# One transformer block on one core: w1 and the last V are summed in 64-row tiles, in two passes with the row halves swapped

## The chip, the cores and the metric

The kernel runs on one core of one Trainium2 chip. The metric is device time in microseconds (us), smaller is better. Before the change three runs took 169.43, 171.04 and 171.4 us; the median is 171.04 us.

The engines of the core are TensorE (PE for its matmuls, PEld for the loads of their stationary operand), VectorE (DVE), ScalarE (ACT), GpSimd (POOL) and SyncE (SP, which here issues the DMAs). Each engine works through its own list of instructions in order, and they wait for each other through semaphores.

## The reference

S is 2048, D is 448, there are 16 heads of 28, and F is 1792. `c` is turned into six modulation vectors of 448.

```python
h = _layernorm(x) * (1 + ca) + sa
x = x + ga * attention(h, wqkv, wo)       # each position sees 8 keys at distances 0, 2, .., 14
h = _layernorm(x) * (1 + cb) + sb
y = _layernorm(h)
x = x + gb * (gelu(y @ w1 + b1) @ w2 + b2)
```

Every product of a 448-wide row with a matrix (q, k, v, w1) sums over 448 = 3 * 128 + 64 rows of the stationary operand. The product with w2 sums over 1792 = 14 * 128.

## The kernel before

The even and the odd positions are two streams (`n` or `s`, 0 and 1), each 1024 long, so a dilated window is an ordinary window inside one stream. A `p` (0 to 7) is 128 positions of both streams, a `t` (0 to 3) is two of these.

The work has three stretches that repeat. **The front** (to about 63 us) loads x and the weights, normalises, forms hT (the transposed rows), q, k and v, and runs attention for the first five of nine batches. **Attention** of a batch `i` is `pv` (v), two `lt` (logits), an exp on ACT, a mask on DVE, `pd` (denominators), `po` (values) and a multiplication on DVE. `out_proj` of a `p` (tile `pw`) adds to x and normalises again into `yT`. **The MLP** of a `t` has fourteen `p1` sums (w1: seven pairs g, of which each has two outputs a in the two banks of one PSUM tile), one GELU on ACT for each output, which writes a slice of `hm`, and then `p2` (w2). Four MLPs follow each other, with the attention batches left over between the first three.

How 448 rows are summed: a matmul over 128 rows uses the whole array. For the last 64 rows the two halves of the array work at the same time: one matmul takes rows 0 to 63 for one output and another takes rows 64 to 127 for the other output. That is the tile shape 64x128 instead of 128x128. `summed()` does this: `full()` (line 548) issues three 128-row matmuls for each output, `rest()` (line 554) one 64-row matmul for each output, side by side in pairs. The operands' 64 last rows lie in both halves for this (`w1_r`, and the last part of `yT` and `hT`).

What sets the order: every piece of work is a task of a `Plan` with its engine, inputs and buffers. The order in which tasks are written out is the list `ORDER`, and the buffer of each tile is in the list `SLOTS`; both are fixed numbers in the file. The PSUM has four tiles of two banks (room "P"), shared by all of pq, pv, lt, pd, po, pw, p1 and p2. A task `12:A` of ORDER runs on ACT instead of its usual engine.

Lines of the profile that the text below names: 548 (128-row matmuls of q, k, v, w1), 554 (their 64-row matmuls), 706 (`pv` of the first five batches), 738 (`lt`), 760 (`pd`), 771 (`po`), 803 (`pw`), 883 (`p2`), 864 (GELU), 609 (q and k out of PSUM), 504 (hT), 661 (w2 scaled by gb on DVE), 456 and 458 (statistics), 469 (a power on POOL), 478 (normalisation), 819 (modulation), 889 (last sum). A program has shortened tile names in the profile: `p` is p1 at lines 548 and 554 and p2 at line 883, `w_s` is w1_s or w2_s, `w_r` is w1_r, `h` is h2.

Of the kernel before, what the change touches and what calls it, by code (L numbers as in the profile page):

```python
# [57 lines left out]
192 273:A 162 157 189 171 308:D 194 172 283 193 244 218 173 195 163 219 158 275 284 196 216 285 167 217 286 447:P 246
197 164 168 165 228 174 169:D 274 309 312 276:D 277 220 313 310 314 166 221 229 225 230 311 224 222:D 247 170 315 245
176 317 316 175 226 248 233 232 318 227 290 249 289:A 319 43 287:A 223 288 320 234 250 558:P 46 45 559 321 47 231 253  # L60
345 342 346 251 560 303 482:P 44 252 324 343 322 291 561 254 323 325 347 326 344 292 304 255 293 327 348 328 373:R 256
305 294 329 257 350 258 375 52 378 376 330 340:R 53 333 379 235 377 374 296 334 331 300 41 295 351 332 259 49 335 380
299 341 336 337 297 260 382 262 301 381 349 263 261 264 338:A 383 483 352 339 384 265 484 266 449 353 267 485 385 268
# [3 lines left out]
402 452 404 443 487 453 370 490 454 444 436 455 371:D 372 456 434 491 405 488 457 493 445 459 458 492 460 435 494 461  # L67
# [3 lines left out]
513 547 515:D 599 516 564 602 568 481 569 570 604 603 571 546 605 572 548 606 573 628 607 608 574 549 635 575 550 609  # L71
612 636 577 630 637 578 610 629 640 576 579 638 581 639 611 613 580 582 641 631 583 633 586 651 614 632 587 584 585
616 588 642 615 648 617 654 646 647 618 634 652 645 656 621 649 619 644 622 620 623 643 658 650 625 624 589 626 664
590 655 627 591:A 653 657 439 592 659 556 665 662 663 674 666 660 661 669 667 675 668 678 676 679 677 686 672 673 671
687 681 670 680 690 691 694 697 693 682 688 692 685 695 683 689 701 684 698 696 709 699 710 702 711 712 705 700 703
706 704 707 708
# [77 lines left out]
def kernel(  # L154
# [14 lines left out]
    nc = tc.nc  # L169
# [3 lines left out]
    P = Plan()  # L173
# [368 lines left out]

    def summed(items, slot, reads, bufs, fills, name, after=(), split=None):
# [70 lines left out]
    def natural_qk(p):  # L614
        c0 = LEAD + 128 * p
        for half in (1, 0):
            pq = psum("pq")

            def item(s, half=half, pq=pq):
                return (lambda: pq.t[:, s, 0:D], lambda kt, rows: hT[rows, NS * kt + s, c0:c0 + 128],  # L620
                        lambda kt, rows: (wqk_st.t[:, kt] if kt < KT - 1 else wqr_st.t[rows])[:, half * D:half * D + D])

            summed([item(s) for s in range(NS)], 0.1895, [f"wqk{k}" for k in range(KT - 1)] + ["wr0", "wr1"] + [f"h{kt}_{p}" for kt in range(KT)],
                   [pq, wqk_st, wqr_st], [pq], f"qk{p}_{half}n")
# [53 lines left out]
    def attention(i, tbl, prev_w1):  # L678
# [5 lines left out]
        if i not in DIRECT:  # L684
# [10 lines left out]
            summed([(lambda s=s: pv.t[:, s, 0:D], lambda kt, rows, s=s: hw.t[rows, kt, s].rearrange("p j c -> p (j c)"),  # L695
# [101 lines left out]
    def out_proj(p):  # L797
        pw = psum("pw")

        def mm():  # L800
            for s in range(NS):
                for ft in range(4):
                    nc.tensor.matmul(pw.t[:, s, 0:D], lhsT=qT[:, KT * s + ft, LEAD + 128 * p:LEAD + 128 * p + 128], rhs=wo_s[:, ft, :],  # L803
                                     start=(ft == 0), stop=(ft == 3))

        batches = [i for i in range(NB) if i * SBQ < 128 * (p + 1) and (i + 1) * SBQ > 128 * p]
        add("PE", 8 * 0.1895, mm, reads=["wos0", "wos1"] + [f"o{i}" for i in batches], bufs=[pw], fills=[pw],
            instr=16, name=f"wo{p}")
# [36 lines left out]
    def mlp(t, tbl, lts):  # L845
        yT = yT_of[t]
        hm = sb("hm", [128, FT, NS, 256], BF16, "hm")
        for gs in ((0, 1), (2, 3), (4, 5), (6,)):
            p1s = {g: psum("p1") for g in gs}

            def item(g, a, p1s=p1s):
                def lhs(kt, rows):
                    c0 = (g + FH * a) * 128
                    return w1_s[rows, kt, c0:c0 + 128] if kt < KT - 1 else w1_r[rows, g * 128:g * 128 + 128]

                return lambda: p1s[g].t[:, a, :], lhs, lambda kt, rows: yT.t[rows, kt:kt + KT + 1:KT, :]

            w1_mms.extend(summed([item(g, a) for g in gs for a in range(2)], 0.2160,
                                 [f"w1{k}" for k in (0, 1, 2, "r0", "r1")] + [(yT, 0), (yT, 1)],
                                 [yT] + list(p1s.values()), list(p1s.values()), f"w1_{t}_{gs[0]}", after=lts))  # L860
# [10 lines left out]
        for q in range(2):  # L871
# [5 lines left out]
            for ns, c0, c1 in (([0], 0, D), ([1], 0, D // 2), ([1], D // 2, D)) if last else (([0, 1], 0, D),):  # L877
                p2, n0, n1 = psum("p2"), ns[0], ns[-1] + 1
                for n in ns:
                    for k, fs in enumerate(parts):  # L880
                        def mm(n=n, fs=fs, q=q, p2=p2, c0=c0, c1=c1):
                            for f in fs:
                                nc.tensor.matmul(p2.t[:, n, 0:c1 - c0], lhsT=hm.t[:, f, n, q * 128:(q + 1) * 128], rhs=w2_s[:, f, c0:c1],  # L883
                                                 start=(f == parts[0][0]), stop=(f == parts[-1][-1]))

                        add("PE", len(fs) * ((c1 - c0) / 2400 + 0.0025), mm, reads=[(hm, f) for f in fs] + [f"w2_{i}" for i in sorted({f // 2 for f in fs})],
                            bufs=[hm, p2], writes=[(p2, n)], instr=2 * len(fs), name=f"w2_{p}_{n}_{k}" + ("b" if c0 else ""))
# [3 lines left out]
                    bufs=[p2, x1p], reads=[(p2, n) for n in ns] + [(x1p, n) for n in ns], writes=[f"out{p}{n0}{c0}"] + ([] if last else [f"x{p}"]), name="fin")  # L891
# [71 lines left out]
```

## Time and profile before

| | |
|---|---|
| time, three runs | 169.43, 171.04, 171.4 us (median 171.04) |
| span of the profiled execution, first to last instruction | 166.6 us |
| PE busy | 160.9 us (97%) in 2126 matmuls |
| DVE busy | 116.1 us (70%) |
| ACT busy | 102.4 us (61%) |
| POOL busy | 46.7 us (28%) |
| TensorE clock granted, mean | 0.998 |

The profile covers one execution. Its span is its own time, as far as the profile gives one; what the timed runs have beyond it (171.04 - 166.6 = 4.4 us at the median) lies around the span. Busy time is the union of an engine's instructions. Matmuls overlap: each is shown from its start to the end of its results, some 0.38 us for 512 columns, while the next one starts 0.216 us after it. So the distance between two starts is what a matmul costs, not its shown duration.

### The profile page before, as it was taken

How to read it: one execution, taken by the hardware profiler on the slowest of the kernel's cores; microseconds unless marked ns; L12 is line 12 of the kernel's file. 1: busy time of each engine (PE TensorE's matmuls, PEld its weight loads, DVE VectorE, ACT ScalarE, POOL GpSimd, SP SyncE). 2: the span in 40 equal slices, each digit the busy share in tenths (PEclk: the TensorE clock that was granted, in tenths of full speed). 3: DMA queues.
4: the chain of work that ended last, by engine and by line, in shares of the span. 5: the costliest groups of instructions: out<-in, count | busy, mean ns of one | idle time of the engine just before them, and what ended most of it. 6: DMA issues, size and time to landing. Idle time of an engine off the chain costs nothing.

```text
span 166.6 us, 4971 instructions
## 1 busy us (share of the span) xinstructions
PE 160.9 (97%) x2126; PEld 83.7 (50%) x2126; DVE 116.1 (70%) x271; ACT 102.4 (61%) x142; POOL 46.7 (28%) x73
## 2 busy tenths in 40 slices
PE   6999899999999999999999999999999999999992
PEld 4678544444545543445555344556434455344572
DVE  6889899958899989996938886574788930500032
ACT  3378898798489953859674468947536820097300
POOL 3136332300261201289100114700002870007200
PEclk9999999999999999999999999999999999999999
DMA  5999989799999999900091000009010026110003
GB/s 152 323 335 311 182 269 172 147 160 190 222 185 306 147 161 245 151 0 6 2 139 46 4 0 0 4 0 126 8 55 0 0 55 185 64 46 0 0 1 110
DMA packets 35573, 18.78 MB, mean 113 GB/s; under 512 B 28507, under 2 KB 34592, under 8 KB 35552
## 3 DMA queue, kind: packets, MB, share of 16 engines
q1 hardware_dynamic: 35548, 18.47, 51.0%
q8 instruction: 16, 0.26, 0.7%
q14 instruction: 5, 0.04, 0.1%
q10 hardware_dynamic: 4, 0.00, 0.0%
HBM read 9.81 MB, written 1.84 MB: 70 GB/s over the span
## 4 chain that ended last, share of the span: by engine, by line
PE 88%; DMA 4%; ACT 2%; SPq 2%; POOL 1%; DVE 1%; issue 1%
PE p L883 26%; PE p L548 22%; PE pq L548 8%; PE pw L803 8%; PE pv L706 5%; PE p L554 4%; PE lt L738 4%; PE po L771 3%; PE pv L548 3%; DMA wqk_st<-in_A_wqkv_dram 3%; PE pq L554 2%; DMA kT<-zy 2%; PE pd L760 1%; SPq L349 1%; PE pb L641 1%
## 5 line engine op out<-in xcount | busy, mean ns | idle before, releaser
L864 ACT ACTIVATE hm<-p,b_col 128x512 bf16<-128x512 f32 x56 | 33.9, 692 | 29.9 <-PE p L554 27.3
L883 PE MATMUL p<-w_s,hm 128*128 128x448 bf16 (+1 forms) x238 | 44.1, 342 | 0.0
L548 PE MATMUL p<-yT,w_s 128*128 128x512 bf16 x168 | 38.1, 380 | 0.0
L469 POOL TENSOR_TENSOR rs_all<-mvs,neg_half 128x2 f32<-128x2 f32 x22 | 16.7, 764 | 58.0 <-DVE mvs L458 57.9
L883 PEld LDWEIGHTS <-hm 128*128 128x128 bf16 x238 | 22.6, 98 | 19.3 <-issue 0.8
L889 DVE TENSOR_TENSOR x_all<-p,x1p 128x896 bf16<-128x896 f32 (+2 forms) x10 | 8.9, 902 | 25.9 <-PE p L883 25.9
L548 PEld LDWEIGHTS <-w_s 128*128 128x128 bf16 x168 | 15.8, 98 | 20.9 <-issue 2.9
L456 DVE BATCH_NORM_STATS2 stt<-x_all 128x6 f32<-128x448 bf16 x32 | 18.6, 608 | 0.8 <-DMA x_all<-in_A_x_dram 0.6
L745 ACT ACTIVATE et<-lt 128x928 bf16<-128x928 f32 x18 | 16.0, 947 | 4.2 <-PE lt L738 3.9
L841 POOL TENSOR_TENSOR x1p<-x_all,gbb_bc 128x448 f32<-128x448 bf16 x16 | 17.8, 1137 | 0.0
L548 PE MATMUL pq<-wqk_st,hT 128*128 128x448 bf16 x72 | 15.0, 354 | 0.0
L788 DVE TENSOR_TENSOR qT<-po,den 128x912 bf16<-128x912 f32 x9 | 10.0, 1106 | 6.6 <-ACT den L782 6.4
L751 DVE TENSOR_TENSOR et<-et,mask 128x928 bf16<-128x928 bf16 x18 | 11.8, 683 | 3.1 <-ACT et L745 3.0
L803 PE MATMUL pw<-wo_s,qT 128*128 128x448 bf16 x64 | 13.3, 353 | 0.0
L780 ACT ACTIVATE den<-pd 128x928 f32<-128x928 f32 x9 | 8.5, 943 | 5.9 <-PE pd L760 5.7
L819 DVE TENSOR_TENSOR h<-h,mod_bc 128x896 bf16<-128x896 bf16 x16 | 11.1, 710 | 0.3
L628 ACT CAST zy<-pq 128x896 bf16<-128x896 f32 x10 | 8.9, 912 | 1.7 <-PE pq L554 0.9
L548 PEld LDWEIGHTS <-hT 128*128 128x128 bf16 x72 | 6.4, 98 | 6.9 <-issue 1.6
L782 ACT ACTIVATE den<-den,den_bias 128x928 f32<-128x928 f32 x9 | 9.6, 1072 | 0.2
L478 DVE TENSOR_SCALAR zy<-h,mvs,rs_all 128x448 bf16<-128x448 bf16 x16 | 6.6, 457 | 4.4 <-POOL rs_all L469 4.4
L810 DVE TENSOR_TENSOR x_all<-pw,x_all 128x896 bf16<-128x896 f32 x8 | 8.7, 1086 | 1.3 <-PE pw L803 1.3
L456 DVE BATCH_NORM_STATS2 stt<-h 128x6 f32<-128x448 bf16 x16 | 9.4, 612 | 0.2
(115 smaller groups left out, 182.0 us busy)
## 6 DMA issues: line engine op xcount, KB each, us to landing
w_s<-in_B_w_dram SPq DMA_DIRECT2D x7, 224.0 KB, 3.8
out_dram<-x_all SPq DMA_DIRECT2D x7, 224.0 KB, 2.1
x_all<-in_A_x_dram SPq DMA_DIRECT2D x3, 448.0 KB, 5.3
wmod<-in_w_mod_dram SPq DMA_DIRECT2D x3, 448.0 KB, 7.2
w_s<-in_B_w_dram SPq DMA_DIRECT2D x3, 448.0 KB
wqk_st<-in_A_wqkv_dram SPq DMA_DIRECT2D x3, 225.0 KB, 3.9
wm_st<-in_w_mod_dram SPq DMA_DIRECT2D x1, 672.0 KB, 4.6
x_all<-in_A_x_dram SPq DMA_DIRECT2D x2, 224.0 KB, 2.6
```

The costliest lines, as they stand in the source:

```text
L456: add("DVE", 0.53, lambda: nc.vector.bn_stats(out=stt[:, w, b, 0:6], in_=src()), reads=reads, bufs=bufs, after=early if w == b == 0 else ( ...
L469: ways = {"POOL": (0.55 + 0.17 * n, lambda: nc.gpsimd.tensor_tensor(out=r, in0=v, in1=neg_half[:, 0:n], op=ALU.pow))}
L548: nc.tensor.matmul(out(), lhsT=lhs(kt, slice(0, 128)), rhs=rhs(kt, slice(0, 128)), start=first and kt == 0, stop=not first and kt == KT - 2)
L554: nc.tensor.matmul(out(), lhsT=lhs(KT - 1, rows), rhs=rhs(KT - 1, rows), start=first, stop=not first, tile_position=(rows.start, 0))
L745: exps.append(add("ACT", 0.83, lambda half=half, lt=lt: nc.scalar.activation(out=et.t[:, 2 * half:2 * half + 2].rearrange("p r m c -> p r ...
L751: nc.vector.tensor_tensor(out=ev, in0=ev, in1=mask[:], op=ALU.mult)
L788: nc.vector.tensor_tensor(out=qT[:, :, LEAD + q00:LEAD + q00 + 2 * WQ], in0=po.t[:, :, 0:NS * 4 * WQ].rearrange("p j (m c) -> p m j c", c=WQ),
L803: nc.tensor.matmul(pw.t[:, s, 0:D], lhsT=qT[:, KT * s + ft, LEAD + 128 * p:LEAD + 128 * p + 128], rhs=wo_s[:, ft, :], start=(ft == 0), sto ...
L819: add("DVE", 0.55, lambda vec=vec, op=op: nc.vector.tensor_tensor(out=h2.t[:], in0=h2.t[:], in1=vec.unsqueeze(1).to_broadcast([128, NS, D] ...
L841: add("POOL", 1.0, lambda n=n: nc.gpsimd.tensor_tensor(out=x1p.t[:, n, :], in0=xn(p, n), in1=gbb2_bc[:], op=ALU.add), reads=[f"x{p}", "gbb ...
L864: gelus.append(add("ACT", 0.585, lambda f=f, a=a, p1=p1s[g]: nc.scalar.activation(out=hm.t[:, f].rearrange("p n c -> p (n c)"), in_=p1.t[: ...
L883: nc.tensor.matmul(p2.t[:, n, 0:c1 - c0], lhsT=hm.t[:, f, n, q * 128:(q + 1) * 128], rhs=w2_s[:, f, c0:c1], start=(f == parts[0][0]), stop ...
```

## The change

`paired()` takes the place of `summed()` for all w1 sums (two outputs each) and for the v of the last batch (`PAIRED_V = range(8, 9)`). All of its matmuls have the tile shape 64x128, two side by side. In the first pass, rows 0 to 63 work for output 0 and rows 64 to 127 for output 1, over all four parts of the 448 rows (the last part lies in both halves): 8 matmuls. In the second pass the halves change places, over the first three parts: 6 matmuls. Each output has then seen each of its rows once.

[...] For this there is a "hop": an instruction without work on SP, POOL, ACT or DVE that waits for the last matmul of the first pass and then signals; the first weight load of the second pass waits for that signal. ORDER says on which engine each hop runs. There are 29: 8 on DVE, 8 on POOL, 8 on SP, 5 on ACT. Between the two passes of one sum stands work of other sums.

```diff
+PAIRED_QK, PAIRED_V, PAIRED_WO, PAIRED_W2 = range(0), range(8, 9), range(0), range(0)
...
+    def swapped(first, bufs, second):
+        ends = []
+        def hop(e):
+            nop = e.nop()
+            for mm in ends:
+                link(mm, nop)
+            ends.append(nop)
+        a = first(ends)
+        b = add("SP", 0.05, lambda: hop(nc.sync), needs=a, name="hop", alt={"POOL": (0.05, lambda: hop(nc.gpsimd)), "ACT": (0.05, lambda: hop(nc.scalar)),
+                                                                           "DVE": (0.05, lambda: hop(nc.vector))})
+        return a + second(ends, [b])
...
+    def paired(items, slot, reads, bufs, fills, name, after=(), rest=True):
+        n = KT - 1 if rest else KT
+        seen = []
+        def half(first, ends):
+            start, mm = not seen, None
+            seen.append(1)
+            for kt in range(KT if first else n):
+                for a in range(2):
+                    out, lhs, rhs = items[a if first else 1 - a]
+                    rows = slice(KS * a, KS * a + KS)
+                    mm = nc.tensor.matmul(out(), lhsT=lhs(kt, rows), rhs=rhs(kt, rows), start=start and kt == 0,
+                                          stop=not start and kt == n - 1, tile_position=(rows.start, 0))
+                    if not first and kt == a == 0:
+                        link(ends[-1], mm)
+            if first:
+                ends.append(mm)
...
-            summed([(lambda s=s: pv.t[:, s, 0:D], lambda kt, rows, s=s: hw.t[rows, kt, s].rearrange("p j c -> p (j c)"),
+            (paired if i in PAIRED_V else summed)([(lambda s=s: pv.t[:, s, 0:D], lambda kt, rows, s=s: hw.t[rows, kt, s].rearrange("p j c -> p (j c)"),
...
-            w1_mms.extend(summed([item(g, a) for g in gs for a in range(2)], 0.2160,
+            for g in gs:
+                w1_mms.extend(paired([item(g, a) for a in range(2)], 0.2160, [f"w1{k}" for k in (0, 1, 2, "r0", "r1")] + [(yT, 0), (yT, 1)],
+                                     [yT, p1s[g]], [p1s[g]], f"w1_{t}_{g}", after=lts))
```

The same function could be used for q and k, for `pw` and for `p2`; those switches are empty ranges, so there the program is built as before. ORDER and SLOTS are new numbers throughout, and the order has moved on every engine. In the line numbers of the changed kernel, 548 is 592, 554 is 598, the matmuls of `paired()` are 576, the hop is 551, 609 is 653, 661 is 705, 706 is 750, 738 is 782, 864 is 915, 883 is 957 and 889 is 963.

**PE at the first MLP.** Before, around the first w1 sums (`p1_1587`, `p1_1594`, `p1_1613`; 1534 is the number of this yT):

```order
L548 LDWEIGHTS w1_s_76 [waits DMAHW5_49,DMAHW4_49,DMAHW7_49]
L548 MATMUL p1_1587<-yT_1534,w1_s_76 128x512 [waits Activation_49]
...
L548 MATMUL p1_1594<-yT_1534,w1_s_76 128x512 [waits DVE_49]
...
L554 LDWEIGHTS w1_r_77 [waits DMAHW1_49]
L554 MATMUL p1_1613<-yT_1534,w1_r_77 128x512 [waits DVE_49]
...
L548 MATMUL p1_1613<-yT_1534,w1_s_76 128x512
```

Now, at the same place (`p1_1580`, `p1_1593`, `p1_1608`; all tile shape 64x128):

```order
L576 MATMUL p1_1608<-yT_1524,w1_s_76 128x512
L576 LDWEIGHTS w1_r_77
L576 MATMUL p1_1608<-yT_1524,w1_r_77 128x512
L576 LDWEIGHTS w1_s_76 [waits Pool_sequencer_49]
L576 MATMUL p1_1580<-yT_1524,w1_s_76 128x512
...
L576 LDWEIGHTS w1_s_76 [waits DVE_sequencer_49]
L576 MATMUL p1_1593<-yT_1524,w1_s_76 128x512
```

Before, twelve 128-row matmuls, then eight 64-row ones, then 128-row ones again: two changes of shape. Now the first passes of 1580, 1593 and 1608 stand behind each other, then the second pass of 1580, whose first weight load waits for the hop on POOL, then that of 1593, which waits for the hop on DVE; the shape does not change.

**DVE during the first MLP.** Before, from the sum behind the last `pw` on (L810; `w2_s` rows scale two of the fourteen slices of w2 each):

```order
L810 TENSOR_TENSOR x_all_68<-pw_1570,x_all_68 128x896 [waits PE_49]
...
L661 TENSOR_TENSOR w2_s_78<-w2_s_78,mod_bc_82 128x896 [waits DMAHW7_49]
...
L456 BN_STATS stt_105<-h2_1607 128x6 [waits DVE_49]
L478 TENSOR_SCALAR h2_1665<-x_all_68,mvs_106,rs_all_107 128x448 [waits Pool_49]
...
L661 TENSOR_TENSOR w2_s_78<-w2_s_78,mod_bc_82 128x896 [waits DMAHW2_49]
```

Now, around its second hop (the hop itself is not a row; its wait for PE is listed with the row behind it):

```order
L733 COPY hw_1629<-hT_69 128x1024 [waits PE_49]
...
L481 TENSOR_SCALAR h2_1656<-x_all_68,mvs_106,rs_all_107 128x448 [waits Pool_49]
L705 TENSOR_TENSOR w2_s_78<-w2_s_78,mod_bc_82 128x896 [waits PE_49,DMAHW4_49]
L481 TENSOR_SCALAR h2_1643<-x_all_68,mvs_106,rs_all_107 128x448
L870 TENSOR_TENSOR h2_1643<-h2_1643,mod_bc_82 128x896 [waits DVE_49]
L705 TENSOR_TENSOR w2_s_78<-w2_s_78,mod_bc_82 128x896 [waits DMAHW7_49]
...
L705 TENSOR_TENSOR w2_s_78<-w2_s_78,mod_bc_82 128x896 [waits DMAHW1_49]
```

In both the scaling of w2 is mixed with the normalisation for the next MLP. Now DVE has two hops in it: one ahead of the copy into `hw_1629` (after the first pass of `p1_1593`) and one ahead of the scaling that waits for DMAHW4 (after the first pass of `p1_1667`). Seven scalings there are in both; three come ahead of the second hop and four behind it.

**PE in the front.** Before, at the q and k of the second `p` (`pq_353`, `pq_362`) and the start of attention (`lt_391`, `pv_447`):

```order
L548 MATMUL pq_362<-hT_69,Wqk_72 128x256
...
L554 MATMUL pq_362<-hT_69,Wqr_73 128x256
L554 MATMUL pq_353<-hT_69,Wqr_73 128x256
...
L738 MATMUL lt_391<-qT_70,kT_71 64x58 [waits PE_49]
...
L548 MATMUL pq_353<-hT_69,Wqk_72 128x256
...
L706 MATMUL pv_447<-Wv_74,hT_69 64x448 [waits Activation_49]
```

Now, at the same place (`pq_350`, `pq_365`, `lt_376`, `lt_410`, `pv_482`):

```order
L598 MATMUL pq_350<-hT_69,Wqr_73 128x256
...
L598 MATMUL pq_365<-hT_69,Wqr_73 128x256
...
L782 MATMUL lt_376<-qT_70,kT_71 64x58 [waits Activation_49]
...
L782 MATMUL lt_410<-qT_70,kT_71 64x58
...
L592 MATMUL pq_365<-hT_69,Wqk_72 128x256
...
L750 MATMUL pv_482<-Wv_74,hT_69 64x448 [waits Activation_49]
```

The two `lt` of the first batch now stand together, and ahead of them there are six 128-row matmuls and two pairs fewer; those come behind them. On ACT, `kT` is now copied out ahead of `qT`, and two parts of hT for the third `p` are formed there instead of one.

More of the change, by code (lines that the diff above doesn't have):

```diff
@@ L58 @@
[L58 to L62, printed above, removed]
@@ L77 @@
+732:P 725 738 714 728 743 739:A 715 744 740 729:D 745 733 730 746 736 748 737 747 734 742 762 735 750 741 749 763 751
+754 752 764 753 755 765 758 756 759 757 760 761
 """
@@ L620, in item @@
                 return (lambda: pq.t[:, s, 0:D], lambda kt, rows: hT[rows, NS * kt + s, c0:c0 + 128],
-                        lambda kt, rows: (wqk_st.t[:, kt] if kt < KT - 1 else wqr_st.t[rows])[:, half * D:half * D + D])
-            summed([item(s) for s in range(NS)], 0.1895, [f"wqk{k}" for k in range(KT - 1)] + ["wr0", "wr1"] + [f"h{kt}_{p}" for kt in range(KT)],
+                        lambda kt, rows: (wqk_st.t[rows, kt] if kt < KT - 1 else wqr_st.t[rows])[:, half * D:half * D + D])
+            (paired if p in PAIRED_QK else summed)([item(s) for s in range(NS)], 0.1895, [f"wqk{k}" for k in range(KT - 1)] + ["wr0", "wr1"] + [f"h{kt}_{p}" for kt in range(KT)],
                    [pq, wqk_st, wqr_st], [pq], f"qk{p}_{half}n")
@@ L798, in out_proj, with item @@
         pw = psum("pw")
+        def item(s):
+            return (lambda: pw.t[:, s, 0:D], lambda ft, rows: qT[rows, KT * s + ft, LEAD + 128 * p:LEAD + 128 * p + 128],
+                    lambda ft, rows: wo_s[rows, ft, :])
         def mm():
             for s in range(NS):
+                out, lhs, rhs = item(s)
                 for ft in range(4):
-                    nc.tensor.matmul(pw.t[:, s, 0:D], lhsT=qT[:, KT * s + ft, LEAD + 128 * p:LEAD + 128 * p + 128], rhs=wo_s[:, ft, :],
-                                     start=(ft == 0), stop=(ft == 3))
+                    nc.tensor.matmul(out(), lhsT=lhs(ft, slice(0, 128)), rhs=rhs(ft, slice(0, 128)), start=(ft == 0), stop=(ft == 3))
         batches = [i for i in range(NB) if i * SBQ < 128 * (p + 1) and (i + 1) * SBQ > 128 * p]
-        add("PE", 8 * 0.1895, mm, reads=["wos0", "wos1"] + [f"o{i}" for i in batches], bufs=[pw], fills=[pw],
-            instr=16, name=f"wo{p}")
+        reads = ["wos0", "wos1"] + [f"o{i}" for i in batches]
+        if p in PAIRED_WO:
+            paired([item(s) for s in range(NS)], 0.1895, reads, [pw], [pw], f"wo{p}", rest=False)
+        else:
+            add("PE", 8 * 0.1895, mm, reads=reads, bufs=[pw], fills=[pw], instr=16, name=f"wo{p}")
         xp = x_all[:, p, :].rearrange("p (s d) -> p s d", s=NS)
@@ L878, in mlp, with sums, half, mm @@
                 p2, n0, n1 = psum("p2"), ns[0], ns[-1] + 1
[L879 to L887, printed above, removed]
+                if p in PAIRED_W2:
+                    count = []
+                    def sums(k, up, ends, q=q, p2=p2, count=count):
+                        mm, fs, done = None, parts[k], len(count)
+                        count.append(k)
+                        for f in fs:
+                            for a in range(2):
+                                n, rows = (1 - a if up else a), slice(KS * a, KS * a + KS)
+                                mm = nc.tensor.matmul(p2.t[:, n, 0:D], lhsT=hm.t[rows, f, n, q * 128:(q + 1) * 128], rhs=w2_s[rows, f, :],
+                                                      start=done == 0 and f == fs[0], stop=done == 3 and f == fs[-1], tile_position=(rows.start, 0))
+                                if done == 2 and f == fs[0] and a == 0:
+                                    link(ends[-1], mm)
+                        if done == 1:
+                            ends.append(mm)
+                    def half(up, ends, needs=(), p=p, p2=p2, sums=sums):
+                        return [add("PE", len(parts[k]) * 0.1895, lambda k=k, sums=sums: sums(k, up, ends), instr=4 * len(parts[k]), mode="64x128", needs=needs,
+                                    reads=[(hm, f) for f in parts[k]] + [f"w2_{i}" for i in sorted({f // 2 for f in parts[k]})],
+                                    bufs=[hm, p2], joins=[p2], name=f"w2_{p}_{'lh'[up]}{k}") for k in range(2)]
+                    swapped(lambda ends: half(False, ends), [p2], lambda ends, b: half(True, ends, b))
+                else:
+                    for n in ns:
+                        for k, fs in enumerate(parts):
+                            def mm(n=n, fs=fs, q=q, p2=p2, c0=c0, c1=c1):
+                                for f in fs:
+                                    nc.tensor.matmul(p2.t[:, n, 0:c1 - c0], lhsT=hm.t[:, f, n, q * 128:(q + 1) * 128], rhs=w2_s[:, f, c0:c1],
+                                                     start=(f == parts[0][0]), stop=(f == parts[-1][-1]))
+                            add("PE", len(fs) * ((c1 - c0) / 2400 + 0.0025), mm, reads=[(hm, f) for f in fs] + [f"w2_{i}" for i in sorted({f // 2 for f in fs})],
+                                bufs=[hm, p2], writes=[(p2, n)], instr=2 * len(fs), name=f"w2_{p}_{n}_{k}" + ("b" if c0 else ""))
@@ L890, in mlp @@
                     out=xo(xi), in0=p2.t[:, n0:n1, 0:w], in1=xo(x1p.t), op=ALU.add),
-                    bufs=[p2, x1p], reads=[(p2, n) for n in ns] + [(x1p, n) for n in ns], writes=[f"out{p}{n0}{c0}"] + ([] if last else [f"x{p}"]), name="fin")
+                    bufs=[p2, x1p], reads=[(p2, n) for n in ns if p not in PAIRED_W2] + [(x1p, n) for n in ns], writes=[f"out{p}{n0}{c0}"] + ([] if last else [f"x{p}"]), name="fin")
                 lo, hi = n0 * D + c0, (n1 - 1) * D + c1
```

42 lines of the change are left out of this document (28 added, 14 removed), and 18 rows, old and new, of tables (ORDER, SLOTS).

## The prediction

> **What bounds the kernel now.** I read the head of the page first, then the busy times by stretch, then the waits, and only then single stretches of the timeline.
>
> ```profile
> span 166.6 us, 4971 instructions
> PE 160.9 (97%) x2126; PEld 83.7 (50%) x2126; DVE 116.1 (70%) x271; ACT 102.4 (61%) x142; POOL 46.7 (28%) x73
> ```
>
> PE is busy for all but 5.7 us of the span. The stretches (start:end, length, then PE, PEld, DVE, ACT and POOL busy, clock granted, DMA share, GB/s) say where these 5.7 us are:
>
> ```profile
> 0.00:12.40 12.40, 10.61 (x108) 7.66 (x108) 9.81 (x52) 5.57 (x13) 3.54 (x15) 1.00 0.87 269
> 12.40:29.00 16.60, 16.05 (x336) 9.72 (x335) 15.55 (x44) 14.07 (x20) 6.26 (x13) 1.00 1.00 236
> 29.00:45.00 16.00, 15.60 (x331) 7.75 (x332) 12.98 (x21) 11.94 (x14) 2.43 (x3) 1.00 0.91 174
> 45.00:62.90 17.90, 17.89 (x334) 9.11 (x321) 16.92 (x40) 15.52 (x19) 4.75 (x6) 1.00 1.04 202
> 62.90:73.90 11.00, 11.00 (x58) 4.46 (x56) 10.85 (x25) 5.85 (x10) 4.20 (x6) 1.00 0.81 144
> ...
> 153.00:166.60 13.60, 10.65 (x71) 6.59 (x68) 2.50 (x4) 2.44 (x5) 2.03 (x3) 0.98 0.10 34
> ```
>
> 1.79 us lie in the first 12.4 us, where weights arrive and which the change does not touch; 0.55 + 0.40 + 0.01 = 0.96 us in the rest of the front; none from 62.9 to 153; 2.95 us behind the last matmul. So nothing but the length of PE's own stream, and those 0.96 us, can be shortened. The longest wait of the front is the only one over 0.4 us:
>
> ```profile
> PE pv L706 <- ACT qT L609: 0.5, 1, 0.5
> ```
>
> **The stream of w1.** Twelve 128-row matmuls in a row, and a place where the shape changes:
>
> ```profile
> 94.76 2.75 PE L548 MATMUL p<-yT,w_s 128*128 128x512 bf16 x12
> ...
> 64.74 0.81 PE L548 MATMUL p<-yT,w_s 128*128 128x512 bf16 x3
> 65.49 1.04 PE L554 MATMUL p<-yT,w_r 64*128 64x512 bf16 x8
> 66.45 0.39 PE L548 MATMUL p<-yT,w_s 128*128 128x512 bf16 x1
> ```
>
> The last of the twelve takes 0.38 us to the end of its results (a group's mean of 380 ns stands in a row below), so the other eleven lie (2.75 - 0.38) / 11 = 0.2155 us apart. I call this a slot. Three matmuls should take 0.647 us, but the next group starts 0.75 us after them; four pairs should take 0.862 us, but take 0.96. So a pair of 64-row matmuls costs one slot, and **each change of shape about 0.10 us** more (0.095 when it is averaged over more of them).
>
> Before, two outputs cost 2 x 3 full slots and one pair: 7 slots. Now they cost (8 + 6) / 2 = 7 pair slots. For 28 pairs of outputs that is 28 x 7 x 0.2155 = 42.2 us both times: the new shape saves nothing by itself, and the 174 further matmuls (w1 392 for 224, the last V 14 for 8) lie in the other half of the same slots. What it does save is changes of shape. Counted in the order of PE's two programs there are 79 before and 73 now: seven fewer in the MLPs, one more in the front. **Term 1: -6 x 0.095 = -0.57 us.** It is small because the 64-row blocks of w1 were already collected to three or four pairs. Bounds: -0.6 to 0; zero if the pairs lose as much in another way.
>
> That pairs keep the pace over more than four of them is not shown for 64-row tiles, but for another half tile, 128x64, whose sixteen matmuls start at 20.01 and whose successor starts at 21.58 (rows further down): 1.57 us for eight pairs of 448 columns, against 8 x 0.2155 x 448/512 = 1.51 and one change of shape. The same row of instructions can be taken quickly enough:
>
> ```profile
> 84.09 1.21 PE po L771 x128
> ```
>
> That is 9.4 ns for each matmul with its weight load. [...]
>
> **The hops.** A second pass starts when the first has ended, another engine has noticed, and PE has noticed that. Each step from its row:
>
> ```profile
> L548 PE MATMUL p<-yT,w_s 128*128 128x512 bf16 x168 | 38.1, 380 | 0.0
> ...
> 163.68 0.39 DVE L889 TENSOR_TENSOR x_all<-p,x1p 128x224 bf16<-128x224 f32 x1 [0.72 <-PE p L883]
> ...
> 153.02 10.64 PE p L883 x70
> ```
>
> 0.38 us to the results; 153.02 + 10.64 = 163.66 to 163.68, 0.02 us from PE's end to another engine's start; and (rows below) ACT's cast from 17.01 to 18.02, PE's `pv` at 18.07: 0.05 us back. The hop itself does no work; I put its own time at 0.02 to 0.06 us by the shortest DVE rows, an estimate. So some **0.49 us** from the start of the last matmul of a first pass to the first weight load of the second. By the new order, seven of the 29 hops have three slots of other w1 work between the passes (0.65 us), seven have four (0.86 us), fifteen have six or more. A load may come up to one slot ahead of its matmul, so an undisturbed hop has at least 0.16 us to spare and costs nothing: the cover is the other sums' slots. If this cover were gone, a hop would cost 0.49 - 0.2155 = 0.27 us, 29 of them 8 us.
>
> But a hop stands in its engine's queue, and ahead of it may be an instruction of 0.7 to 1.1 us. Of the fourteen short ones five are on SP, four on DVE, three on POOL, two on ACT. Between 62.9 and 73.9 us ACT is busy 5.85 and POOL 4.20 of 11 us, DVE 10.85. So I charge DVE's four: half of a 0.73 us instruction (0.36) less the spare 0.16 to 0.37 gives about 0.1 each, and SP's five, which may stand behind a DMA's issue, little less. **Term 2: +0.25 us** for all, which is near the lower end; bounds 0 and +4 (all fourteen 0.3 us late).
>
> **DVE in the first MLP.** Here it was full, and w2 has to be scaled in time:
>
> ```profile
> 72.60 1.15 DVE L661 TENSOR_TENSOR w_s<-w_s,mod_bc 128x896 bf16<-128x896 bf16 x2
> 73.80 0.73 PE L883 MATMUL p<-w_s,hm 128*128 128x448 bf16 x3
> ```
>
> The last scalings ended at 73.75 and the first w2 matmul began at 73.80, without delay. Now DVE stands still at its second hop until the first pass of `p1_1667` is done. What follows it, up to the sixth scaling, is three scalings, two normalisations and two modulations:
>
> ```profile
> L661 DVE TENSOR_TENSOR w_s<-w_s,mod_bc 128x896 bf16<-128x896 bf16 x7 | 4.9, 726 | 0.0
> L478 DVE TENSOR_SCALAR h<-x_all,mvs,rs_all 128x448 bf16<-128x448 bf16 x16 | 5.8, 384 | 1.8 <-POOL rs_all L469 1.6
> L819 DVE TENSOR_TENSOR h<-h,mod_bc 128x896 bf16<-128x896 bf16 x16 | 11.1, 710 | 0.3
> ```
>
> 3 x 0.726 + 2 x 0.384 + 2 x 0.710 = 4.37 us, begun 0.42 us after the last matmul's start, so ready for PE at 4.84. PE has twenty pair slots (4.31 us), 32 small `lt` matmuls (0.37) and two changes of shape (0.19) behind that slot before the first w2: 0.22 + 4.87 = 5.09. **Term 3: 0**, with 0.25 us to spare. Bounds 0 and +1.4.
>
> **The front.** PE and ACT around the first attention, before:
>
> ```profile
> 14.70 0.49 PE L548 MATMUL pq<-hT,Wqk 128*128 128x256 bf16 x3
> 15.12 0.61 PE L554 MATMUL pq<-hT,Wqr 64*128 64x256 bf16 x8
> 15.66 0.44 PE L738 MATMUL lt<-qT,kT 28*64 28x58 bf16 x32
> 16.04 1.48 PE L548 MATMUL pq<-hT,Wqk 128*128 128x256 bf16 x12
> 18.07 1.64 PE L706 MATMUL pv<-Wv,hT 128*64 128x448 bf16 x16 [0.55 <-ACT qT L609]
> 19.64 0.44 PE L738 MATMUL lt<-qT,kT 28*64 28x58 bf16 x32
> 20.01 1.64 PE L706 MATMUL pv<-Wv,hT 128*64 128x448 bf16 x16
> 21.58 0.70 PE L738 MATMUL lt<-qT,kT 28*64 28x58 bf16 x64
> ...
> 13.55 1.02 ACT L609 CAST qT<-pq 128x1024 bf16<-128x1024 f32 x1
> 14.44 1.04 ACT L609 CAST kT<-pq 128x1024 bf16<-128x1024 f32 x1
> 17.01 1.01 ACT L609 CAST qT<-pq 128x1024 bf16<-128x1024 f32 x1
> 21.40 0.81 ACT L504 ACTIVATE hT<-zT,mod_col 128x512 bf16<-128x512 bf16 x1
> ```
>
> The first `lt` needs both casts, which end at 15.48; it started at 15.66, so it hardly waited. Now six 128-row matmuls and two pairs of 256 columns fewer stand ahead of it, 8 x 0.108 = 0.87 us (0.108 is half a slot). It is up at 14.79 and must wait to 15.53: 0.74 us new. The 0.87 us of work come behind it and use up what was the 0.55 us wait at 18.07; what is left at that `pv` is 0.74 - 0.55, some +0.15. Then the second part of hT that ACT now forms (0.81 us, in a stretch where ACT is busy 14.07 of 16.60) makes the next q and k late by what I put at 0.3. **Term 4: +0.4 us.** Bounds: -0.55, if the `pv` wait goes and nothing takes its place, and 0.74 + 0.3 = +1.0. The last V's two passes have four slots between them and cost nothing by the same cover as w1.
>
> **The sum:** -0.57 + 0.25 + 0 + 0.4 = +0.1 us. The profiled span becomes 166.7; with the 4.4 us by which the median stands above the span, 171.1 us. The tail (w2, last sum, store) is as it was.
>
> **The rivals.**
>
> - *Hops come late (slower).* An engine passes a hop only when what stands ahead of it has finished, so that PE, which never waited between 62.9 and 153 us, now does. For it: DVE's 10.85 of 11.00. Against it: ACT and POOL are half idle, and 15 hops have 1.3 us or more. Price 14 x 0.3 = +4.2 in place of 0.25: 175 us. It decides from a mean lateness of 0.24 us at these fourteen on. Chance 0.10.
> - *DVE's hop holds back w2.* The 1.4 us in which DVE stands still are not made up, and the first w2 matmul waits for a scaling: +1.3, 172.4 us. For it: no slack before; against it: the 0.25 us above. Chance 0.09.
> - *The front's waits go.* All of the 0.96 us vanish and hops are free: -0.57 - 0.96 = -1.5, 169.5 us. Chance 0.10.
> - [...] Chance 0.01.
> - *Faster by more than 2%.* 3.4 us, which is about what a measurement of this kernel can tell from no change, would need more than all waits and all the changes of shape that go (1.5 us): something I do not see. Chance 0.04.
>
> The forecast has the remaining 0.66. The range: from 169.5 with 0.8 us for the spread of the runs (169.43 to 171.4) down to 168.7, and from 172.4 with the front at its upper bound (+0.6) and a few late hops up to 173.5. Slower by over 2% takes the late hops and the slow pace, 0.11; within 2% the forecast, w2 and the front, 0.85.
>
> **What would show it.** Changes of shape: in the MLPs PE's stretches of w1 come out some 0.14 us shorter each. Hops: PE waits on SP, DVE, POOL or ACT at the `paired` line, in sum about 0.25 us; over 3 us of them is the first rival. w2: a wait of the first `p2` for DVE. Front: a wait of 0.7 us at the first `lt` instead of that at `pv`. I am wrong if a long run of 64-row pairs does not keep 0.2155 us for a slot, or if engines pass hops much later than they pass waits now.

## The result: 3% slower, and the profile after

Four runs of the changed kernel took 175.01 to 176.63 us, median 175.24, beside 170.71 for the kernel before: a ratio of **1.031 (95% interval 1.025 to 1.037)**. The forecast was 171.1, its range 168.7 to 173.5. The time lies where the first rival put it (175), but not for that rival's reason, so that this is luck.

The head of the page of the changed kernel, and its busy times by stretch (the columns are as in the prediction):

```profile
span 173.0 us, 5358 instructions
...
PE 160.9 (93%) x2300; PEld 84.3 (49%) x2300; DVE 119.3 (69%) x271; ACT 103.2 (60%) x144; POOL 46.3 (27%) x71
```

```profile
12.40:29.00 16.60, 14.59 (x250) 8.45 (x252) 13.86 (x43) 12.98 (x19) 5.97 (x11) 1.00 0.93 209
29.00:45.00 16.00, 14.69 (x355) 7.88 (x354) 12.19 (x20) 13.13 (x16) 0.64 (x2) 1.00 0.97 164
45.00:66.87 21.87, 20.73 (x384) 10.04 (x384) 20.94 (x42) 15.35 (x18) 5.74 (x7) 1.00 0.87 169
...
76.90:98.90 22.00, 20.11 (x374) 10.54 (x372) 17.08 (x28) 12.59 (x15) 8.33 (x8) 1.00 0.31 47
...
108.50:126.40 17.90, 17.47 (x350) 9.31 (x348) 12.56 (x22) 12.45 (x14) 7.20 (x9) 1.00 0.27 32
...
137.20:148.50 11.30, 10.62 (x56) 5.29 (x55) 5.84 (x11) 3.74 (x7) 3.02 (x4) 1.00 0.53 88
148.50:159.20 10.70, 10.70 (x99) 4.71 (x100) 1.51 (x2) 5.51 (x9) 2.75 (x4) 1.00 0.17 64
```

PE's busy time is the same 160.9 us. The whole loss of 6.4 us of span is time in which PE stands still: 2.0 + 1.3 + 1.1 us in the front, where it was 0.96, and 1.9 + 0.4 + 0.7 us behind it, where it was nothing. The fourth w1 (the last row) has no idle time and is shorter, 10.70 us for 11.00. Before:

```profile
142.00:153.00 11.00, 11.00 (x58) 4.54 (x56) 2.09 (x2) 6.08 (x10) 2.14 (x4) 1.00 0.11 42
```

What PE waited for, by line (us in total, times, longest):

```profile
PE pd L804 <- DVE et L795: 1.6, 2, 1.1
PE pq L592 <- ACT hT L507: 1.3, 1, 1.3
...
PE pw L852 <- DVE qT L832: 0.8, 1, 0.8
PE p L957 <- issue: 0.7, 1, 0.7
PE p L576 <- DMA yT<-zy: 0.7, 1, 0.7
PE lt L782 <- ACT qT L653: 0.7, 1, 0.7
PE pq L598 <- DVE vb L768: 0.7, 1, 0.7
PE lt L782 <- DMA qT<-zy: 0.6, 1, 0.6
```

No wait for a hop is among them: the only wait of the paired line 576 is for `yT`, at the start of the fourth MLP. Instead the engines that carry hops waited for PE:

```profile
POOL rs_all L472 <- PE p L576: 2.0, 1, 2.0
DVE w_s L705 <- PE p L576: 1.8, 1, 1.8
DVE mvs L461 <- PE p L576: 1.5, 1, 1.5
```

From the starts of matmuls in the traces:

| us | before | after | difference |
|---|---|---|---|
| first w1 matmul (end of the front) | 62.80 | 66.71 | +3.9 |
| from there to the first w1 matmul of the fourth MLP | 79.06 | 81.80 | +2.7 |
| from there to the end of the last matmul | 21.79 | 21.49 | -0.3 |

These differences compare two single executions. The text ahead of the prediction puts all of the 4.4 us by which the median time of before exceeds its profiled span outside the span. The later runs list time and span of every execution, and there only 1.7 us lie outside it (2.0 for the changed kernel). The executions of before have spans from 166.4 us up, with a median of 168.2 to 168.6 us in each set of runs: the profiled one is among the shortest. The four of the changed kernel have a median of 173.25 us. So between medians the loss is some 4.9 us instead of 6.4: the trace of before lies 1.6 to 2.0 us below its median, that of the changed kernel 0.25.

In the front there is no hop at all; it was only reordered. So three questions follow: what the front lost, what the middle lost, and what the pairs cost by themselves.

### The profile page after: what moved, and what is told of

It is laid out like the page before. It is cut to its first block, busy times and chain, and to the rows that moved or that the text cites. A ratio compares the mean times of both kernels' runs of the same rounds, so it can differ in the third digit from the quotient of the medians.

```text
span 173.0 us, 5358 instructions
## 1 busy us (share of the span) xinstructions
PE 160.9 (93%) x2300; PEld 84.3 (49%) x2300; DVE 119.3 (69%) x271; ACT 103.2 (60%) x144; POOL 46.3 (27%) x71
## 4 chain that ended last, share of the span: by engine, by line
PE 44%; DVE 23%; DMA 10%; ACT 7%; issue 6%; POOL 6%; SPq 2%; POOLq 0%; DVEq 0%; ACTq 0%
PE p L576 20%; PE p L957 11%; DVE stt L459 5%; PE pw L852 3%; DVE et L795 3%; DVE h L870 3%; POOL rs_all L472 3%; DVE zy L481 3%; DMA yT<-zy 3%; DMA wqk_st<-in_A_wqkv_dram 2%; DMA mod_bc<-mod_hbm 2%; DMA zT<-zy 2%; PE pq L592 2%; ACT hT L507 2%; PE po L815 2%
## 5 line engine op out<-in xcount | busy, mean ns | idle before, releaser
L576 PE MATMUL p<-yT,w_s 64*128 64x512 bf16 x336 | 41.5, 376 | 0.7 <-DMA yT<-zy 0.7
L576 PEld LDWEIGHTS <-w_s 64*128 64x128 bf16 x336 | 16.2, 94 | 20.6 <-DMA yT<-zy 1.1
L892 POOL TENSOR_TENSOR x1p<-x_all,gbb_bc 128x448 f32<-128x448 bf16 x16 | 18.4, 1171 | 0.1
L795 DVE TENSOR_TENSOR et<-et,mask 128x928 bf16<-128x928 bf16 x18 | 12.6, 723 | 4.2 <-ACT et L789 4.2
L870 DVE TENSOR_TENSOR h<-h,mod_bc 128x896 bf16<-128x896 bf16 x16 | 12.5, 780 | 0.4
L765 ACT CAST vb<-pv 128x896 bf16<-128x896 f32 x7 | 6.2, 901 | 7.8 <-PE pv L576 5.1
L576 PE MATMUL p<-yT,w_r 64*128 64x512 bf16 x56 | 10.6, 376 | 0.0
L852 PEld LDWEIGHTS <-qT 128*128 128x128 bf16 x64 | 6.1, 98 | 7.3 <-DVE qT L832 1.9
```

The source lines that it names most:

```text
L576: mm = nc.tensor.matmul(out(), lhsT=lhs(kt, rows), rhs=rhs(kt, rows), start=start and kt == 0, stop=not start and kt == n - 1, tile_positi ...
L795: nc.vector.tensor_tensor(out=ev, in0=ev, in1=mask[:], op=ALU.mult)
L852: nc.tensor.matmul(out(), lhsT=lhs(ft, slice(0, 128)), rhs=rhs(ft, slice(0, 128)), start=(ft == 0), stop=(ft == 3))
L870: add("DVE", 0.55, lambda vec=vec, op=op: nc.vector.tensor_tensor(out=h2.t[:], in0=h2.t[:], in1=vec.unsqueeze(1).to_broadcast([128, NS, D] ...
L892: add("POOL", 1.0, lambda n=n: nc.gpsimd.tensor_tensor(out=x1p.t[:, n, :], in0=xn(p, n), in1=gbb2_bc[:], op=ALU.add), reads=[f"x{p}", "gbb ...
```

## Experiments

In the short diffs of the order, the names are tasks: `w1_2_4f` and `r` are the 128-row and the 64-row block of w1 (third MLP, pairs 4 and 5), `p` and `q` the first and second pass of one pair.

**1. The front.** Everything up to the first w1 in the order and buffers of before, the rest as changed:

```diff
-ORDER, SLOTS up to w1_0_0p: as in the changed kernel
+ORDER, SLOTS up to w1_0_0p: as before the change
```

> The front (all up to the first w1 matmul) in the order and buffers of before, everything from the first w1 on as in the changed kernel. Theory A1 (3.8 us were lost in the front, by its order, where there is no hop): first w1 near 63 us instead of 66.7, span 169 to 169.6 us, ratio to before 1.014 to 1.02. Rival D (what the front loses the rest would have lost in any case, because the same chains of normalisation end late): span 172 us or more.

Ratio to before 1.028 (1.014 to 1.041), above the 1.014 to 1.020 that were expected; span 168.9 us. The first w1 matmul, before, in this kernel and in the changed one (start, time, count of the group):

```profile
62.80 1.46 PE L548 MATMUL p<-yT,w_s 128*128 128x512 bf16 x6
```

```profile
62.19 0.82 PE L571 MATMUL p<-yT,w_s 64*128 64x512 bf16 x6
```

```profile
66.71 0.59 PE L576 MATMUL p<-yT,w_s 64*128 64x512 bf16 x4
```

The profile gives the 4 us back, and the rest then needs what it needed in the changed kernel (82.2 us to the fourth MLP for 81.8). But this is the shortest of the four executions (168.9 to 173.3 us): between the medians of the spans the gain is 2.1 us (173.25 to 171.15), and the timed ratio is too wide to say so by itself; experiment 5 has a second timed pair. The old front is also less steady than one trace suggests: over the eight traces of this study that have it at a granted clock of 0.98 or more, before included, w1 begins at 62.2 to 65.5 us (median 63.7), with the new front at 66.6 to 68.6 us in six (median 67.1). By these medians the new front costs some 3.4 us.

In this kernel one hop did hold up PE, in the first MLP (546 is the hop's line here, on DVE):

```profile
PE p L571 <- DVEq L546: 0.5, 1, 0.5
```

From start to start that is 0.7 us beyond a slot. The changed kernel has no such row.

**2. One piece of the front.** Where I had looked for the wait of q and k at 24 us, the trace shows that the fourth `p`'s statistics now stand between those of the third:

```diff
-144 135 133 142 134 136 145 143 139 278 147 138 140 148    (DVE; 133 to 139 are the third p)
+135 133 144 134 136 142 145 143 139 138 140 147 148 278
```

> The changed kernel with one edit in the front: on DVE the statistics and normalisations of the third p come one after the other ahead of those of the fourth, as before the change, and one statistics instruction of a later p moves behind them. Theory A1 (part of the front's 3.8 us is zT for the third p, which came at 22.4 us instead of 20.3): the transposes are issued at 15.5 instead of 16.85, the 1.5 us wait of the q and k at 24.1 falls to 0.2 or less, span 171.6 to 172.2 us. Rival D (another wait takes its place, since DVE, ACT and PE wait for each other all along the front): less than 0.5 us gained.

```profile
15.52 3.10 SPq L530 DMA_TRANSPOSE zT<-zy  x2
```

```profile
23.59 1.69 PE L592 MATMUL pq<-wqk_st,hT 128*128 128x448 bf16 x8 [0.67 <-ACT hT L507]
```

The transposes were issued at 15.52, as expected, and the wait halved (0.67 for 1.34). But the first w1 began at 66.55 instead of 66.71, and the ratio was 1.036 (1.028 to 1.044): rival D. Matmul for matmul the gain was still 0.5 to 0.7 us up to the `lt` at 35.75; then `pw` waited 0.57 us for hT at 43.99, where the changed kernel did not wait, and 0.2 us of the gain were left. The front's loss is no single wait; **which of its moves begins it stays open**.

**3. Hops.** No hops at all, and, in another kernel, all of them on SP (some entries of the order; without a letter a hop runs on SP):

```diff
-            out, lhs, rhs = items[a if first else 1 - a]
+            out, lhs, rhs = items[a]
...
-            if not first and kt == a == 0:
-                link(ends[-1], mm)
```

```diff
-408:P 411:D 418:A 421:D 431:P ...
+408 411 418 421 431 ...
```

> The changed kernel without hops: both passes of a sum use the same row halves (so half of the sum is counted twice and half left out), so no pass has to wait for the other; order, engines, buffers and the number and shape of the matmuls stay. Theory A (the order): the front loses its 3.8 us as before this edit and the middle its 2.7, span 172 to 173 us. Rival C (a hop makes DVE, POOL or ACT stand still, and what stands behind it comes late): the front keeps its 3.8, but the waits of pd for DVE's masks and of the last w1 for yT go, span 170 to 171 us.

> The changed kernel with all 29 hops on SP. Rival C (hops hold up DVE, POOL and ACT): as without hops in the middle, span 170 to 171 us, if SP passes them in time. Theory A (the order): 172.5 to 174 us, DVE's waits for PE at its old hop places gone but the waits of PE as they were. If SP is late with its hops, waits of PE at the paired line stand out, 1 us or more each.

Both kernels were 1.030 of before (intervals 1.022 to 1.038 and 1.020 to 1.040): against the changed kernel's 1.031 the timing cannot resolve the step. The traces show it. From the first to the fourth w1 the changed kernel took 81.80 us and the kernel of experiment 2, with the same hops, 82.05; without hops it was 80.42, with hops on SP 80.59. POOL and DVE in the second MLP, changed kernel:

```profile
105.86 0.69 POOL L472 TENSOR_TENSOR rs_all<-mvs,neg_half 128x2 f32<-128x2 f32 x1 [1.97 <-PE p L576]
```

```profile
106.58 0.40 DVE L481 TENSOR_SCALAR h<-x_all,mvs,rs_all 128x448 bf16<-128x448 bf16 x1 [1.30 <-POOL rs_all L472]
```

and POOL at this place without hops:

```profile
101.81 1.46 POOL L472 TENSOR_TENSOR rs_all<-mvs,neg_half 128x2 f32<-128x2 f32 x2 [11.84 <-DVE mvs L461]
```

Without hops POOL forms both powers one behind the other. With them the second stood behind a hop, which waited 1.97 us for PE; DVE then waited 1.30 us for the power; the normalisations, masks and the next `yT` came later. In the changed kernel PE then waited 0.6 us at `pd` (117.5) and 0.85 us at the fourth w1 (148.5); both waits are gone in both kernels. **In the changed kernel a hop cost PE nothing where it stood, and the hops cost 1.2 to 1.4 us in all through what was queued behind them.** Every kernel here that swaps the halves has hops, so no run shows what a second pass without one would do.

On SP the hops made the stretch from the first w1 to the first w2 0.4 us longer (11.44 for 11.04): twice PE took 0.39 us for a slot, for the hop was late.

**4. Masks beside POOL.** What stayed without hops was 1.3 us at the first `pd`. Its masks on DVE, and what POOL did then:

```profile
83.60 3.39 DVE L795 TENSOR_TENSOR et<-et,mask 128x928 bf16<-128x928 bf16 x3
```

```profile
83.70 2.79 POOL L892 TENSOR_TENSOR x1p<-x_all,gbb_bc 128x448 f32<-128x448 bf16 x2
```

```profile
87.05 0.59 PE L804 MATMUL pd<-et,ones_k 64*32 64x464 bf16 x16 [1.15 <-DVE et L795]
```

Three masks in 3.39 us: the raw instructions are 0.60, 1.48 and 1.47 us long, and the long ones began while an `x1p` ran. Each of them ended 0.50 us behind the end of that `x1p`; the short one had begun 0.10 us ahead of it. Before the change seventeen of eighteen masks took 0.60 to 0.78 us, and the only long one (1.45) began during an `x1p` too and ended 0.50 us behind it. So I moved the two additions behind POOL's next power:

```diff
-368 444 443 401    (POOL; 368 and 401 are powers, 444 and 443 x1p)
+368 401 444 443
```

> The changed kernel with one edit in the first MLP: the two additions x1p on POOL that ran beside the masks of attention on DVE (83.7 to 86.5 us) move behind POOL's next power. In the trace a mask took 0.64 us alone and 1.47 us beside x1p. If this contention made pd wait 1.3 us: masks of 0.6 us, no wait of pd, span 171.7 to 172.3 us. Rival E (the masks were late because exp was late): masks as short, but pd waits 0.8 us or more, span within 0.5 us of the changed kernel. If x1p slows what it now stands beside (normalisations), 0.5 us or so comes back.

```profile
84.24 1.70 DVE L795 TENSOR_TENSOR et<-et,mask 128x928 bf16<-128x928 bf16 x3
```

Three masks in 1.70 us, and this wait of `pd` is gone. From the first to the fourth w1 it took 79.80 us, 2.0 less than the changed kernel: 1.3 at `pd`, 0.7 at the fourth `yT`. The wait for that `yT` was gone without hops too (experiment 3), so it needed both causes and can't be put down to one of them. Ratio 1.027 (1.020 to 1.034), span 171.9, within the expected 171.7 to 172.3; the times alone don't resolve the step from 1.031. By the lengths of the masks it is the contention, not a late exp.

The instruction that began first was not slowed: the mask that began 0.10 us ahead of an `x1p` took 0.60 us, and before the change the `x1p` in which the mask of 1.45 us began took 1.03 us, the one ahead of it 1.04. Why the later of the two takes longer, no run shows.

**5. Do the causes add up?** The old front and hops on SP together; then the move of `x1p` as well:

> Two edits of the changed kernel at once: the front in the order and buffers of before, and all hops on SP. If the front's order (3.7 to 4.1 us by the last runs) and the engines made to wait by hops (0.85 + 0.6 us of waits for yT and for a mask, which went without hops) are separate causes, they add: span 167.2 to 167.9 us, ratio 1.00 to 1.01; what is left over before is the wait of pd for masks in the first MLP (1.3 us). If they overlap: 168.5 us or more.

> Three edits of the changed kernel together: the front in the order of before, all hops on SP, and the two x1p of the first MLP behind POOL's next power. If the three causes add (front 3.7 to 4.1, hops that hold up POOL and DVE 1.2, masks beside x1p 0.9 us): span 166.8 to 167.6 us but for PE's stops without a wait (0.6 to 2 us), ratio 1.000 to 1.010. If they overlap or another chain takes over: span over 169 us, ratio over 1.015.

Ratio 1.011 (1.004 to 1.019) for the first. That is 1.9% (3.2 us) below the same kernel with the new front (1.030, 1.020 to 1.040), and the intervals just miss each other. The medians of the times, 174.15 and 171.90 us, lie 2.3 us apart. Together with experiment 1 this puts the timed size of the front's loss at 2.1 to 3.2 us. The span was 170.7, not 167.2 to 167.9, with 1.2 us lost in the first 19 us and 2.3 us of stops without a wait (0.5 before). With `x1p` too, the ratio was **1.001 (0.997 to 1.006)**, within the expected 1.000 to 1.010; of this kernel only the times are used, for its profiled execution had a granted clock of 0.95. The three edits undo the whole loss, though all other moves of the new order and all 29 hops are still there.

**6. The pairs by themselves.** The order and buffers of before, with w1 and the last V in pairs. It took me three versions:

```diff
-w1_0_2f w1_0_0r w1_0_2r w1_0_0f gelu ...
+w1_0_2p hop:A w1_0_3p hop:A w1_0_2q gelu gelu w1_0_1p hop:A w1_0_3q gelu gelu ...    (third version)
```

> The paired sums and their hops alone: order and buffers of before, only the w1 sums (and the last V) in two passes, first pass of a pair, second pass of the pair before, and so on, so that seven slots (1.5 us) lie between the passes of a pair; all hops on ACT. Theory A (the new order lost the time, not the pairs): PE waits as in before, fewer changes of shape, span 165.7 to 166.6 us, ratio to before 0.995 to 1.00. Rival B (the pairs or the hops cost by themselves): span 169 to 173 us with waits or longer distances at the paired line, ratio 1.015 to 1.04.

Ratio 1.076 (1.063 to 1.089): a miss of my own making. Hops stood ahead of GELUs on ACT, and PE waited for PSUM tiles that these GELUs had to empty:

```profile
160.91 1.47 PE L571 MATMUL p<-yT,w_s 64*128 64x512 bf16 x6 [3.19 <-ACT hm L910]
```

It is experiment 3's mechanism again, larger: a hop that waits for PE holds up ACT, and PE then waits for ACT.

> Order and buffers of before with the paired sums again (first pass of a pair, second pass of the pair before, and so on; seven slots of other w1 work between the passes of most pairs), but now the two GELUs of a pair stand right behind its second pass in the order, so that no hop on ACT stands ahead of GELUs that are due earlier. In the first version the hops stood ahead of them, the GELUs came late and PE waited 7.9 us for PSUM tiles. Theory A (pairs and hops cost nothing by themselves; the changed kernel lost its time by the order and by what stands behind its hops): span 165.7 to 167 us, ratio to before 0.995 to 1.005. Rival B (pairs or hops cost by themselves): span over 169 us, with waits or longer distances at the paired line.

Ratio 1.027 (1.019 to 1.036): two waits for ACT were left, 2.1 us for the copy of the last v and 1.4 us for a GELU. The new front ahead of this rest gave 1.061 (1.053 to 1.070), a span 7.0 us longer where 3.5 to 4.2 were expected; but w1 began at 68.6 us with 1.2 us of a wait of its own, so it says little on the front:

> The front (all up to the first w1 matmul) as in the changed kernel, the rest in the order of before with the paired sums and hops on ACT. If the front's order alone costs 3.7 us (theory A1): first w1 at 66 to 67 us, span 3.5 to 4.2 us above the kernel with the old order throughout, so 169.5 to 170.5 us. If the rest can take up what the front lost: less than 2 us above it.

> The order of before with the paired sums, third version: the second pass of the last V and its copy out of PSUM stand earlier, and in the fourth MLP the PSUM tiles go round in turn, so that the two waits of the second version (2.1 us for the copy of v, 1.4 us for a GELU) go. Hops on ACT, GELUs behind their second pass. Theory A (pairs and hops cost nothing by themselves): all four stretches of w1 without a wait over 0.4 us, span 165.6 to 166.8 us apart from what PE stands still at the 128 po matmuls (0.3 to 1.3 us in the runs so far, before included), ratio 0.993 to 1.005. Rival B (they do): over 168 us.

Ratio **1.004 (1.000 to 1.009)**: the pairs with 29 hops cost at most 0.9% in a fitting order, and gain nothing. The span of 168.6 us lies in rival B's range, but no wait for a hop is in it: 0.9 us are stops at the `po` and 0.8 us a stop at `p2` (experiment 7). The third and the fourth w1 took 10.71 us each for 11.00, but PE stopped elsewhere.

**7. PE's stops without a wait.** In this kernel as in the changed one:

```profile
88.95 1.31 PE L952 MATMUL p<-w_s,hm 128*128 128x448 bf16 x6 [0.78 <-issue]
```

```profile
92.44 1.29 PE L957 MATMUL p<-w_s,hm 128*128 128x448 bf16 x6 [0.74 <-issue]
```

In all thirteen traces with pairs in the first MLP PE stopped 0.6 to 1.5 us at its matmul number 1500, a little behind the 128 `po`, in two different orders. Before the change there was no stop there. So pairs only in the third and the fourth MLP:

```diff
+            if t in PAIRED_W1:    # range(2, 4)
+                ... paired(...)
+            else:
+                ... summed(...)
```

> The order of before; paired sums only in the third and fourth MLP (hops on ACT), the first two and the last V summed as before. In every kernel with pairs in all MLPs PE stood still without a wait 0.6 to 1.5 us at its matmul 1500, just behind the 128 po of the first MLP, and before there was no such stop. Theory P (the additional instructions of the pairs move this dense place of PE's program to where its instructions come late): none of the 90 additional matmuls lies ahead of this place now, so it stops nowhere between 62 and 110 us, span 165.9 to 166.8 us (four changes of shape fewer than before, -0.4 us), ratio 0.993 to 1.002. Rival Q (the stop comes from something else in the new kernels): it is there still, at some 88 us. If the pairs cost time by themselves in these two MLPs, w1 there takes over 11.0 us each.

```profile
85.62 0.39 PE L799 MATMUL pd<-et,ones_k 64*32 64x464 bf16 x8
85.95 2.44 PE L955 MATMUL p<-w_s,hm 128*128 128x448 bf16 x12
88.23 1.11 PE L847 MATMUL pw<-wo_s,qT 128*128 128x448 bf16 x5
```

No stop: twelve w2 matmuls of 448 columns in 2.44 us. So the stop comes with pairs ahead of this place; whether it is their number or the pairs themselves, this does not separate. The ratio was **0.999 (0.995 to 1.003)**, span 166.7: the fastest kernel with pairs, and not measurably faster than the one before.

**8. The price of a bare hop.** Third and fourth MLP with the second pass right behind the first:

```diff
-w1_2_2p hop:A w1_2_3p hop:A w1_2_2q gelu gelu ...    (second version)
+w1_2_2p hop w1_2_2q gelu gelu w1_2_3p hop w1_2_3q gelu gelu ...
```

> The price of an uncovered hop: as the old order with paired sums, but in the third and fourth MLP the second pass of each pair stands right behind its first pass, with nothing between, and these fourteen hops are on SP. By the prediction's steps (0.49 us from the start of the last matmul of the first pass to the first weight load of the second, less one slot of 0.2155) each costs 0.27 us or, with the weight load itself, up to 0.38: the two stretches of w1 come out 1.9 to 2.7 us longer each. If engines pass hops later (behind DMA issues on SP): 0.5 us or more each, over 3.5 us a stretch.

```profile
152.20 0.38 PE L571 MATMUL p<-yT,w_r 64*128 64x512 bf16 x2
152.68 1.47 PE L571 MATMUL p<-yT,w_s 64*128 64x512 bf16 x12
153.98 0.38 PE L571 MATMUL p<-yT,w_r 64*128 64x512 bf16 x2
154.46 1.47 PE L571 MATMUL p<-yT,w_s 64*128 64x512 bf16 x12
```

From the last matmuls of a first pass (152.20) to the second pass (152.68) lie 0.48 us, all fourteen times the same: 0.26 over a slot. The two stretches took 12.59 us for 10.71, (12.59 - 10.71) / 7 = **0.27 us** a hop. (The times of this single run, 179.65, hold a 2.3 us wait of the second version too.)

## Why the prediction was wrong, by its steps

**What bounds the kernel: right.** Nothing shortened PE's stream but fewer changes of shape, and 160.9 us of PE stayed 160.9.

**Term 1, changes of shape: right in sign, too small.** I put -0.57 us for all, 0.14 for each stretch; the w1 of the third and fourth MLP lost 0.3 us each (11.00 to 10.70). 49 slots are 10.56 us: before, four changes inside them had cost 0.44, now 0.14 is left. Pairs kept the slot over a whole MLP: in the changed kernel the 49 of the fourth w1 start 0.216 us apart in the mean, the shape unchanged throughout. No run shows the slow pace that the prediction's 0.11 for slower counts in.

**Term 2, hops: the price right, the place wrong.** A hop that is not covered costs 0.27 us, as worked out, and in the changed kernel the covered ones cost PE nothing. The sum of this term does not come out by its own words: four hops at 0.1 us and five at little less are 0.8 us, not 0.25. The step that failed is "a hop stands in its engine's queue, and ahead of it may be an instruction": I counted what stands ahead of a hop, as lateness for PE, and not what stands **behind** it. On POOL and DVE the hop itself waited up to 2.0 us, and the normalisation queue behind it came late: 1.2 to 1.4 us. The first rival got the time (175) by luck: its mechanism, PE waiting for late hops, shows no row of 0.2 us in the changed kernel. The mechanism exists, though small: 0.7 us once in experiment 1, twice 0.2 us on SP in experiment 3.

**Term 3, w2 in the first MLP: right.** The first w2 began at 77.75 us without a wait, though DVE stood 1.8 us at its second hop (1.4 were put).

**Term 4, the front: the step that failed and cost most.** I put +0.4 us with bounds of -0.55 and +1.0; it was +3.9 in the two traces, 3.4 between the medians of the traces with either front and 2.1 to 3.2 us by the timed runs. The new wait at the first `lt` was there as worked out (0.68 for 0.74), and the wait at `pv` went. But I took PE and ACT at two places for the whole front and left the orders of DVE and SP unread, where the rows of before (DVE busy 15.55 of 16.60 us) should have warned me that a move there may be paid for. Later waits of 1.5, 0.8, 0.8, 1.0 and 0.5 us (from start to start) were not in the sum. Which of the front's moves begins them stays open.

**Not in the sum at all:** the masks beside `x1p` (1.3 us), which needed the order of POOL against that of DVE, and PE's stop at matmul 1500 (0.9 us from start to start). With 3.9 for the front and 0.6 + 0.85 for the hops these make 7.6 us; the shorter w1 gives back about 1. This adds up the loss between the two traces (6.4 us), of which 1.6 to 2.0 us are the short execution of before.

## What to carry to other kernels

Where an order was searched anew, read the new order of every engine that was nearly full before, not only of the one that bounds the kernel; two places don't stand for a front of 60 us. When a wait is put on another engine's queue, price what stands behind it there; best is an engine with nothing due, or a place behind the work that is due. A saving of 0.3 us in a stretch is lost by one wait of another kind, so see first how large the stretch's own scatter is.

## What the runs showed of the hardware

- A two-input bf16 mask of 128x928 on DVE took 0.60 to 0.64 us in 32 of the 36 cases in the traces of before and of the changed kernel, once 0.78, and 1.45 to 1.48 us in the three cases in which it began while POOL's two-input addition ran (experiment 4). Over all traces twenty masks began so, and each ended 0.50 to 0.53 us behind the addition. Nine began just ahead of one, in its absence, and kept 0.60 to 0.64 us.
- PE's two stops without a wait recur at the same matmuls: among the `po` of the front in eight of the nine kernels with the old front (0.2 to 1.4 us; before the change 0.54 us from the start of matmul 607, at 37.44 us, to the next), and behind matmul 1500 in the thirteen traces with pairs in the first MLP (0.6 to 1.5 us; in the changed kernel 1.09 us from start to start, at 91.35 us). The first place lies in, the second just behind 128 `po` matmuls with their loads, 256 instructions in about 1.2 us. Such a dense stretch alone makes no stop: in the changed kernel the 128 `po` at 57.75 and at 119.44 us start at most 0.10 and 0.16 us apart. The kernel with fewer instructions ahead lost the second stop (experiment 7); what makes PE stop at these places was not measured.
- The old front, in eight traces, ended anywhere from 62.2 to 65.5 us: up to 1.2 us of it lay in the first 19 us, up to 1.4 us in PE's stop among the `po`.
